# Scratch stores issued by POOL instead of the sync engine, and the first score tiles read from the transposed q and k

## The chip, the cores and the metric

The program runs on one core of a Trainium2 chip. The time is device time in microseconds (us). PE is the matrix engine, PEld its weight loads, DVE the vector engine, ACT the scalar engine, POOL the GpSimd engine, and SP the sync engine, which computes nothing and issues DMAs.

## The reference

```python
# attention, batch 4, 8 heads, 576 positions, head size 64, float32
q_rot, k_rot = rotate(q), rotate(k)
scores = q_rot @ k_rot.T / sqrt(64)
attn = softmax(scores)
a = attn @ v                                   # -> x: 2304 tokens x 512
# first layer, d_ff = 1536, weights float64
xn = x / sqrt(mean(x*x) + 1e-6) * rms_g
x = (silu(xn @ w_gate) * (xn @ w_val)) @ w_out
# second layer, d_ff = 1024, weights float64
out = ((x @ w1) * (x @ w2)) @ w3 @ w_out2
```

## The kernel before

**Precision.** A float32 product is made from two parts of each factor, a high part rounded to the fast matmul type and the remainder as the low part, in three passes: high by high, high by low, low by high (`PASS`). Where the contraction is only 64 long (the scores), high and low are stacked over 128 rows, so that two passes give all four products.

**Attention.** It goes over 16 pairs of heads (p = 0 to 15). For each pair POOL rotates q and k, PE transposes them (steps q0p, q1p, q2p), ACT takes the high part into the tile `xy` (q0h, q1h, q2h) and DVE the low part (q0l, q1l, q2l). DMAs issued by SP then move `xy` into the stacks `qs` (q1d, line 434 by `move`) and `ks` (q2d). Nine score tiles per pair follow, t = 0 to 8 (S, line 482): 0 to 3 are the first head's full tiles, 4 holds the left-over rows of both heads, 5 to 8 are the second head's. Each tile has its maximum taken by DVE (M, line 487), its exponential by ACT (E, line 493), is transposed by PE (T, line 499) and split again (H by ACT, Lo by DVE, line 507), before the product with v (PV). The order on every engine is written out by hand in `ORDER`, in units of one score tile. For pair 0 there is a shortcut: the first head's parts of the stacks are not moved by DMA but copied, three casts on ACT (lines 728, 731, 733) and three on DVE (lines 729, 732, 734), so that the first scores do not wait for DMAs; `q1d(0)` and `q2d(0)` then move only what is left (six moves).

**First layer.** Tokens go in six chunks of 384. Each chunk has 12 steps: `pair_mm` (line 305) multiplies by gate and value, `gated` makes the hidden slice (lines 315, 317, 104, 105), and `second` (line 813) adds it, one step later, into the output. Beside these steps run jobs that prepare the second layer. `job_wo`, `job_w3` and `job_ws` load float64 weights (`wraw`), turn them into float32 on ACT and DVE (lines 841 to 846) and store them to scratch tensors in DRAM (`woD`, `w3D`, `wsD`). `job_sums` loads pieces of the finished layer output `x2D`, adds them up as a seven-product (Strassen) scheme wants them, splits them and stores them to `xsD`. Their tiles come from small rings: three buffers for `wraw`, three for `wt`, three for `o`.

**Second layer.** `weights` loads `wsD` as `cf` (line 1024) and splits it into `cw`; `load_xs` loads seven tiles of `xsD` for each of two groups of chunks (line 1075); the third group's tiles are made on the spot from `x2D` (loads `sb`, line 908). `product` multiplies (line 1049), the results go to `uD` (line 1120). Then w3 by w_out2 is multiplied out (line 1152), `uD` is loaded again (line 1161), multiplied (line 1190) and stored to the output.

From the first layer on, a scheduler at build time orders the instructions of each engine. Each engine and each issuing queue then works its list strictly in order: an issue whose source is not ready holds back everything behind it. The DMAs of one issuing engine take turns on eight completion counters, and an issue waits until the DMA that last used its counter has landed. In the kernel before every DMA is issued by SP.

The memory of the `xs` tiles is memory that first-layer weights and inputs had. By the pool sizes in the code, the first three of the seven loads of group 0 (order 0, 1, 4, 5, 6, 2, 3) go into room that the early steps of the last chunk leave free; the fourth needs the room of the last chunk's input `xc`, which the last matmul of line 305 still reads.

Of the kernel before, what the change touches and what calls it, by code (L numbers as in the profile page):

```python
# [60 lines left out]
def f(ap):  # L61
    return ap.bitcast(F32)
# [3 lines left out]
def kernel(  # L66
# [21 lines left out]
    nc = tc.nc  # L88
    B, H, S, D = q.shape
# [346 lines left out]
    @step  # L436
    def q1d(p):
        qs = qst[p % 2]
        sl = slice(0, 640)
        sa = sl  # L440
        if p == 0:
            sa = slice(512, 640)
        move([(qs[0:64, 0, sa], xs[0:64, sa]), (qs[64:128, 0, sa], ys[0:64, sa]),
              (qs[64:128, 1, sl], xs[64:128, sl]), (qs[0:64, 1, sl], ys[64:128, sl])])

    @step
    def q2d(p):
        new_ks(p)
        ks = stacks[p]
        sl = slice(QW, QW + S)  # L450
        move([(ks[a:a + 64, 2 * h:2 * h + 2], xy[64 * h:64 * h + 64, :, sl]) for h in range(1 if p == 0 else 0, 2) for a in (0, 64)])

    def new_ks(p):
        if p not in stacks:
# [15 lines left out]
    def tile_steps(t):  # L470
        def S_(p):
            qs, ks = qst[p % 2], stacks[p]
            ps = ps_s.tile([128, 2, 512], F32, tag="s", name="s")
            if t == 4:
                mm = [(qs[:, h, 512 + 64 * h:640 + 64 * h], ks[:, 2 * h + i]) for h in range(2) for i in range(2)]
            else:
                h, r = hr(t)
                mm = [(qs[:, h, r * 128:(r + 1) * 128], ks[:, 2 * h + i]) for i in range(2)]
            n = len(mm)
            for hf in range(2):  # L480
                for i, (l, r_) in enumerate(mm):
                    nc.tensor.matmul(ps[:, hf, 0:HS], lhsT=l, rhs=r_[:, hf * HS:(hf + 1) * HS], start=(i == 0), stop=(i == n - 1))  # L482
            s_ps[p, t] = ps

        def M_(p):
            nm = s_max[p, t] = sm_p.tile([128, 1], F32, tag="nm", name="nm")
            nc.vector.tensor_reduce(out=nm, in_=s_ps[p, t][:, :, 0:HS], axis=AX.XY, op=ALU.max, negate=True)  # L487

        def E_(p):
            pp = p_sb[p, t] = p_p.tile([128, S], F32, tag="p", name="p")  # L490
            if p not in sums:
                sums[p] = sm_p.tile([128, 9], F32, tag="sums", name="sums")
            nc.scalar.activation(out=pp.rearrange("p (a b) -> p a b", a=2), in_=s_ps.pop((p, t))[:, :, 0:HS], func=AF.Exp,  # L493
                                 bias=s_max.pop((p, t)), scale=1.0, accum_out=sums[p][:, t:t + 1])

        def T_(p):
            ps = t_ps[p, t] = ps_t.tile([128, 4, 128], F32, tag="g", name="tp")
            for c in range(4):
                nc.tensor.transpose(ps[:, c, :], p_sb[p, t][:, LF + c * 128:LF + (c + 1) * 128], idn)  # L499

        def H_(p):
            hi, lo, src = spots(t_ps[p, t], t)
            lastins["act"] = nc.scalar.copy(out=hi, in_=src)  # L503

        def Lo(p):
            hi, lo, src = spots(t_ps.pop((p, t)), t)
            lastins["dve"] = nc.vector.tensor_tensor(out=lo, in0=src, in1=f(hi), op=ALU.subtract)  # L507

        for n_, fn in (("S", S_), ("M", M_), ("E", E_), ("T", T_), ("H", H_), ("Lo", Lo)):
            part[f"{n_}{t}"] = fn  # L510
# [206 lines left out]
            part[n_](0, eng, n)  # L717
    for n_ in ("ra", "rb", "rc", "rd"):
        part[n_](1)
    new_ks(0)  # L720
    ks, sl = stacks[0], slice(QW, QW + S)
    for i, n_ in enumerate(("q2p", "q0p", "q1p")):
        part[n_](0)
        if i < 2:
            warm(i + 1)
    for n_ in ("q2h", "q0h", "q2l", "q0l", "q2d"):
        part[n_](0)
    nc.scalar.copy(out=ks[0:64, 0], in_=xs[0:64, sl])
    nc.vector.tensor_copy(out=ks[0:64, 1], in_=ys[0:64, sl])
    part["q1h"](0), part["q1l"](0)  # L730
    nc.scalar.copy(out=qst[0][0:64, 0, 0:512], in_=xs[0:64, 0:512])
    nc.vector.tensor_copy(out=ks[64:128, 1], in_=ys[0:64, sl])
    nc.scalar.copy(out=ks[64:128, 0], in_=xs[0:64, sl])
    nc.vector.tensor_copy(out=qst[0][64:128, 0, 0:512], in_=ys[0:64, 0:512])
    for n_ in ("q1d", "vh", "vl"):
        part[n_](0)
    load_v(1, x_p.tile([128, 5, 2 * D], F32, tag="x", name="x").rearrange("p r n -> p (r n)").rearrange("p (h n d) -> p h n d", h=2, n=5))
    nc.sync.dma_start(out=g_sb, in_=rms_g.rearrange("(o n) -> o n", o=1).to_broadcast([128, DM]))
# [56 lines left out]
    def part_out():  # L795

        for o in range(KC):
            t = pools["x2"].tile([128, CH], F32, tag="o", name="part")
            (nc.scalar.copy if o % 2 else nc.vector.tensor_copy)(out=t, in_=acc[o][:, 0:CH])
            nc.sync.dma_start(out=part_d[:, o], in_=t)  # L800

    def part_in(o):
        t = pools["x2"].tile([128, CH], F32, tag="o", name="part")
# [3 lines left out]
    def second(kind, i, n, us):  # L807
        first, last_ = [(0, cut - 1), (cut, NF - 1)][n >= cut] if i == 0 else (0, NF - 1)
        if n == first:
            acc_tiles()  # L810
        for o in range(KC):
            for s, (a, b_) in enumerate(PASS):
                nc.tensor.matmul(acc[o][:, 0:CH], lhsT=wo[kind, n][:, a, o * 128:(o + 1) * 128], rhs=us[:, b_],  # L813
                                 start=(n == first and s == 0), stop=(n == last_ and s == 2))
        if n == cut - 1 and i == 0:
            part_out()
        elif n == last_:
            for o in range(KC):
                src = acc[o][:, 0:CH]
                if i == 0:  # L820
                    src = part_in(o)
                    nc.vector.tensor_tensor(out=src, in0=acc[o][:, 0:CH], in1=src, op=ALU.add)
                t = pools["x2"].tile([128, CH], F32, tag="o", name="x2") if i < NCH - 1 else pools["u"].tile([128, CH], F32, tag=("sg", "u", "us", "us")[o], name="x2", bufs=(1, 1, 2, 2)[o])
                nc.scalar.activation(out=t, in_=src, func=AF.Copy, scale=1.0 / UP)
                nc.sync.dma_start(out=x2D[:, o, i * CH:(i + 1) * CH], in_=t)

    def conv(src, c=None):

# [25 lines left out]
    def job_wo(j):  # L854
        load, rest = conv(rows(w_out2, j))

        def go():
            t = rest()
            hi, lo = [wt_p.tile([128, 512], F32R, tag="t", name="wt") for _ in range(2)]
            split(hi, lo, t)  # L860
            for i, o in enumerate((hi, lo)):
                nc.sync.dma_start(out=woD[:, j, i], in_=f(o))
        return [load, go]

    def job_w3(j, h):
        load, rest = conv(rows(w3, j, h))
        return [load, lambda: nc.sync.dma_start(out=w3D[:, j, h], in_=rest())]

    def job_ws(g, s):

        w = (w1, w2)[s]
        cv = [conv(cols(w, 2 * g + i), 1) for i in range(2)]
        u = {}

        def load():
            for ld, _ in cv:
                ld()

        def put(i, t):
            nc.sync.dma_start(out=wsD[:, g, s, i:i + 2].rearrange("p o n -> p (o n)"), in_=t)  # L880

        def go1():
            t1, t2 = [rest() for _, rest in cv]
            u["a"] = a11, a12, a21, a22 = t1[:, 0:256], t1[:, 256:512], t2[:, 0:256], t2[:, 256:512]
            u["s"] = tm = wt_p.tile([128, 512], F32, tag="t", name="wt")
            put(0, t1)
            put(2, t2)
            tt(tm[:, 0:256], a21, a22, ALU.add)
            tt(tm[:, 256:512], tm[:, 0:256], a11)
            put(4, tm)  # L890

        def go2():
            a11, a12, a21, a22 = u["a"]
            tm = u["s"]
            tt(tm[:, 256:512], a12, tm[:, 256:512])
            tt(tm[:, 0:256], a11, a21)
            put(6, tm)
        return [load, go1, go2]
# [31 lines left out]
    def job_sums(P, c):  # L930
        def bufs():
            return ([wst.tile([128, 512, 2], U32, tag="raw", name="wraw").rearrange("p n t -> p (n t)").bitcast(F32)[:, 0:2 * CH] for _ in range(2)],
                    [wt_p.tile([128, 512], F32, tag="t", name="wt")[:, 0:CH] for _ in range(2)])

        def put(i, c, src):
            o = pools["x2"].tile([128, 2, CH], F32R, tag="o", name="xo")
            split(o[:, 0], o[:, 1], src)
            nc.sync.dma_start(out=xsD[:, P, i, :, c], in_=f(o))
        return wsums(P, c, bufs, put)


# [156 lines left out]
    for k, batch in enumerate(todo):  # L1098
# [18 lines left out]
        for st_, b, t, g, s, P in run:  # L1117
            if s:
                nc.vector.scalar_tensor_tensor(out=t[:, 1:4], in0=t[:, 1:4], scalar=UP**-2, in1=G[P][:, 1:4], op0=ALU.mult, op1=ALU.mult)
                nc.sync.dma_start(out=uD[:, 2 * g:2 * g + 2, 2 * P * CH:2 * (P + 1) * CH], in_=t.rearrange("p (g t) n -> p g (t n)", g=2))  # L1120

        g, s, P = batch[-1]
        n_ = (g + 1, s) if P == 2 else None
# [132 lines left out]
```

## Time and profile before

| | |
|---|---|
| median of three runs | 1136.8 us (1135.91 to 1142.46) |
| the profiled execution | 1132.41 us |
| its span, first to last instruction | 1130.6 us |
| mean granted TensorE clock | 0.986 |
| busy in the span | PE 1086.5 us, DVE 691.6, ACT 559.3, POOL 218.6 (nothing after 400 us) |
| DMA packets | 183.52 MB, all but 1.17 MB on the queue fed by SP |

Attention takes about the first 310 us of the span, the first layer runs to 792 us, the second to the end. Times in rows are microseconds from the start of the span. The profile is of one execution, 4.4 us below the median of the runs. A merged row of the timeline (x6) gives the start of its first instruction and the time to the end of its last; what stands in brackets is how long the engine was idle before it and what ended that.

### The profile page before, as it was taken

How to read it: one execution, taken by the hardware profiler on the slowest of the kernel's cores; microseconds unless marked ns; L12 is line 12 of the kernel's file. 1: busy time of each engine (PE TensorE's matmuls, PEld its weight loads, DVE VectorE, ACT ScalarE, POOL GpSimd, SP SyncE). 2: the span in 40 equal slices, each digit the busy share in tenths (PEclk: the TensorE clock that was granted, in tenths of full speed). 3: DMA queues.
4: the chain of work that ended last, by engine and by line, in shares of the span. 5: the costliest groups of instructions: out<-in, count | busy, mean ns of one | idle time of the engine just before them, and what ended most of it. 6: DMA issues, size and time to landing. Idle time of an engine off the chain costs nothing. (4 is left out here: it accounts for less than half of the span.)

```text
span 1130.6 us, 18269 instructions
## 1 busy us (share of the span) xinstructions
PE 1086.5 (96%) x6627; PEld 1042.8 (92%) x6627; DVE 691.6 (61%) x1278; ACT 559.3 (49%) x1241; POOL 218.6 (19%) x191
## 2 busy tenths in 40 slices
PE   6899998999999999999999999999899999999998
PEld 5799998999888999999999999998799999987886
DVE  6999999999889853353677634566353442433221
ACT  4799997899865532232533423332354433323221
POOL 4767877599200000000000000000000000000000
PEclk7999999999999999999999999999999999999999
DMA  7678867685356520150878613866952325703451
GB/s 199 150 188 202 214 162 177 181 208 141 88 183 193 177 93 1 62 172 29 285 243 298 212 43 117 301 185 226 376 182 84 122 84 161 249 15 110 155 168 57
DMA packets 124698, 183.52 MB, mean 162 GB/s; under 512 B 18624, under 2 KB 85696, under 8 KB 124608
## 3 DMA queue, kind: packets, MB, share of 16 engines
q1 hardware_dynamic: 124608, 182.35, 53.1%
q8 instruction: 53, 0.87, 0.3%
q14 instruction: 37, 0.30, 0.1%
HBM read 101.63 MB, written 52.17 MB: 136 GB/s over the span
## 5 line engine op out<-in xcount | busy, mean ns | idle before, releaser
L305 PE MATMUL mm<-xc,wgv 128*128 128x384 f32 x1728 | 319.3, 336 | 1.5 <-ACT wgv L242 0.8
L305 PEld LDWEIGHTS mm<-xc,wgv 128*128 128x128 f32 x1728 | 301.8, 189 | 3.4 <-ACT wgv L242 1.6
L1049 PE MATMUL ps<-xs,cw 128*128 128x384 f32 x1008 | 178.3, 337 | 5.3 <-DMA xs<-xsD 5.2
L1049 PEld LDWEIGHTS ps<-xs,cw 128*128 128x128 f32 x1008 | 176.1, 189 | 7.0 <-DMA xs<-xsD 6.9
L813 PE MATMUL acc<-us,wo 128*128 128x384 f32 x864 | 169.8, 339 | 9.4 <-ACT us L104 6.1
L813 PEld LDWEIGHTS acc<-us,wo 128*128 128x128 f32 x864 | 151.3, 189 | 14.8 <-ACT us L104 8.7
L482 PE MATMUL s<-ks,qs 128*128 128x288 f32 x640 | 122.2, 318 | 11.6 <-ACT p L493 5.1
L493 ACT ACTIVATE p<-s,nm 128x576 f32<-128x576 f32 x144 | 107.5, 746 | 19.4 <-DVE nm L487 18.6
L487 DVE TENSOR_REDUCE nm<-s 128x1 f32<-128x576 f32 x144 | 108.0, 750 | 11.0 <-PE s L482 9.3
L482 PEld LDWEIGHTS s<-ks,qs 128*128 128x128 f32 x640 | 91.6, 193 | 15.4 <-ACT p L493 7.3
L1190 PE MATMUL ps<-wp,us 128*128 128x512 f32 x432 | 98.2, 389 | 1.4 <-ACT us L104 1.4
L1190 PEld LDWEIGHTS ps<-wp,us 128*128 128x128 f32 x432 | 81.0, 188 | 18.6 <-ACT us L104 1.8
L507 DVE TENSOR_TENSOR pt<-tp,pt 128x512 fp32r<-128x512 f32 x144 | 94.6, 682 | 1.3 <-ACT pt L503 0.6
L317 DVE SCALAR_TENSOR_TENSOR u<-mm,sg 128x384 f32<-128x384 f32 x72 | 39.9, 554 | 80.4 <-PE mm L305 72.1
L499 PE MATMUL tp<-idn,p 128*128 128x128 f32 x576 | 83.2, 277 | 0.7 <-DVE lt L537 0.4
L503 ACT CAST pt<-tp 128x512 fp32r<-128x512 f32 x144 | 82.5, 585 | 1.0 <-PE tp L499 0.2
L555 PE MATMUL pv<-pt,vs 128*128 128x288 f32 x512 | 81.9, 302 | 0.9 <-DVE pt L507 0.9
L104 ACT CAST us<-u 128x384 fp32r<-128x384 f32 x72 | 36.9, 512 | 89.2 <-DVE u L317 83.6
L555 PEld LDWEIGHTS pv<-pt,vs 128*128 128x128 f32 x512 | 71.7, 190 | 1.4 <-DVE pt L507 1.4
L499 PEld LDWEIGHTS tp<-idn,p 128*128 128x128 f32 x576 | 68.5, 143 | 2.3 <-PE s L482 0.9
L315 ACT ACTIVATE sg<-mm 128x384 f32<-128x384 f32 x72 | 35.1, 487 | 55.8 <-PE mm L305 55.3
L841 ACT ACTIVATE wraw<-wraw 128x512 f32<-128x512 f32 x40 | 27.5, 689 | 67.2 <-DMA wraw<-in_moe_w_dram 61.6
(138 smaller groups left out, 1352.8 us busy)
## 6 DMA issues: line engine op xcount, KB each, us to landing
ks<-xy SPq DMA_DIRECT2D x62, 288.0 KB, 5.0
wraw<-in_moe_w_dram SPq DMA_DIRECT2D x32, 512.0 KB, 5.2
xsD<-xo SPq DMA_DIRECT2D x28, 384.0 KB, 3.4
xs<-xsD SPq DMA_DIRECT2D x14, 768.0 KB, 9.8
wraw<-in_moe_w_out_dram SPq DMA_DIRECT2D x20, 512.0 KB, 4.8
qs<-xy SPq DMA_DIRECT2D x62, 160.0 KB, 2.8
uD<-gv SPq DMA_DIRECT2D x12, 768.0 KB, 3.9
gv<-uD SPq DMA_DIRECT2D x24, 384.0 KB, 4.4
```

The source lines that it names most:

```text
L305: nc.tensor.matmul(ps[:, 0:CH], lhsT=w[:, a, s, c * 128:(c + 1) * 128], rhs=x[:, b_, c, :], start=(i == 0), stop=(i == 3 * KC - 1))
L317: nc.vector.scalar_tensor_tensor(out=u, in0=va, scalar=1.0 / UP, in1=sg, op0=ALU.mult, op1=ALU.mult)
L482: nc.tensor.matmul(ps[:, hf, 0:HS], lhsT=l, rhs=r_[:, hf * HS:(hf + 1) * HS], start=(i == 0), stop=(i == n - 1))
L487: nc.vector.tensor_reduce(out=nm, in_=s_ps[p, t][:, :, 0:HS], axis=AX.XY, op=ALU.max, negate=True)
L493: nc.scalar.activation(out=pp.rearrange("p (a b) -> p a b", a=2), in_=s_ps.pop((p, t))[:, :, 0:HS], func=AF.Exp, bias=s_max.pop((p, t)), s ...
L499: nc.tensor.transpose(ps[:, c, :], p_sb[p, t][:, LF + c * 128:LF + (c + 1) * 128], idn)
L503: lastins["act"] = nc.scalar.copy(out=hi, in_=src)
L507: lastins["dve"] = nc.vector.tensor_tensor(out=lo, in0=src, in1=f(hi), op=ALU.subtract)
L555: nc.tensor.matmul(ps[:, 0:HS], lhsT=l.rearrange("p s d -> p (s d)"), rhs=r, start=(i == 0), stop=(i == 8))
L813: nc.tensor.matmul(acc[o][:, 0:CH], lhsT=wo[kind, n][:, a, o * 128:(o + 1) * 128], rhs=us[:, b_], start=(n == first and s == 0), stop=(n = ...
L1049: nc.tensor.matmul(b[ch], lhsT=w[i][:, p_, c * 128:(c + 1) * 128], rhs=x[i][:, r, c], start=(first and ch != 1 and n == 0), stop=(n == 5), ...
L1190: nc.tensor.matmul(ac[o], lhsT=us[j // 2][:, a, j % 2, o * 128:(o + 1) * 128], rhs=wp[j][:, b_], start=(j == 0 and s == 0), stop=(j == NJ ...
```

## The change

Two things are changed.

1. All stores to the scratch tensors are issued by POOL: `part_d`, `x2D`, `woD`, `w3D`, `wsD`, `xsD` and `uD` (4, 24, 16, 16, 32, 28 and 12 stores). Loads, the stores of `xD` and of the output, and the moves of `xy` stay with SP.
2. The shortcut of pair 0 is replaced. Score tiles 0 to 3 are multiplied straight from `xy`, 64 rows, in three passes instead of two; the six copies are dropped, and `q1d(0)` and `q2d(0)` move whole stacks, as they do for every other pair (eight moves).

```diff
     def q1d(p):
...
-        if p == 0:
-            sa = slice(512, 640)
-        move([(qs[0:64, 0, sa], xs[0:64, sa]), (qs[64:128, 0, sa], ys[0:64, sa]),
+        move([(qs[0:64, 0, sl], xs[0:64, sl]), (qs[64:128, 0, sl], ys[0:64, sl]),
...
-        move([... for h in range(1 if p == 0 else 0, 2) for a in (0, 64)])
+        move([... for h in range(2) for a in (0, 64)])
...
+            if p == 0 and t < 4:
+                mm = [(xy[0:64, a, o], xy[0:64, b_, QW:QW + S]) for a, b_ in PASS]
...
-    for n_ in ("q2h", "q0h", "q2l", "q0l", "q2d"):
-        part[n_](0)
-    nc.scalar.copy(out=ks[0:64, 0], in_=xs[0:64, sl])
-    nc.vector.tensor_copy(out=ks[0:64, 1], in_=ys[0:64, sl])
-    part["q1h"](0), part["q1l"](0)
-    nc.scalar.copy(out=qst[0][0:64, 0, 0:512], in_=xs[0:64, 0:512])
-    nc.vector.tensor_copy(out=ks[64:128, 1], in_=ys[0:64, sl])
-    nc.scalar.copy(out=ks[64:128, 0], in_=xs[0:64, sl])
-    nc.vector.tensor_copy(out=qst[0][64:128, 0, 0:512], in_=ys[0:64, 0:512])
-    for n_ in ("q1d", "vh", "vl"):
+    for n_ in ("q2h", "q0h", "q2l", "q0l", "q1h", "q1l", "q2d", "q1d", "vh", "vl"):
         part[n_](0)
...
-            nc.sync.dma_start(out=part_d[:, o], in_=t)
+            nc.gpsimd.dma_start(out=part_d[:, o], in_=t)
...
-                nc.sync.dma_start(out=x2D[:, o, i * CH:(i + 1) * CH], in_=t)
+                nc.gpsimd.dma_start(out=x2D[:, o, i * CH:(i + 1) * CH], in_=t)
...
-                nc.sync.dma_start(out=woD[:, j, i], in_=f(o))
+                nc.gpsimd.dma_start(out=woD[:, j, i], in_=f(o))
...
-        return [load, lambda: nc.sync.dma_start(out=w3D[:, j, h], in_=rest())]
+        return [load, lambda: nc.gpsimd.dma_start(out=w3D[:, j, h], in_=rest())]
...
-            nc.sync.dma_start(out=wsD[:, g, s, i:i + 2].rearrange("p o n -> p (o n)"), in_=t)
+            nc.gpsimd.dma_start(out=wsD[:, g, s, i:i + 2].rearrange("p o n -> p (o n)"), in_=t)
...
-            nc.sync.dma_start(out=xsD[:, P, i, :, c], in_=f(o))
+            nc.gpsimd.dma_start(out=xsD[:, P, i, :, c], in_=f(o))
...
-                nc.sync.dma_start(out=uD[:, 2 * g:2 * g + 2, 2 * P * CH:2 * (P + 1) * CH], in_=t.rearrange("p (g t) n -> p g (t n)", g=2))
+                nc.gpsimd.dma_start(out=uD[:, 2 * g:2 * g + 2, 2 * P * CH:2 * (P + 1) * CH], in_=t.rearrange("p (g t) n -> p g (t n)", g=2))
```

## Rows read from the trace of the kernel before

**Rows 1.** Busy time by stretch: us, engine busy (count), PEclk, DMA share, GB/s.
```profile
200.00:300.00 100.00, 98.03 (x786) 95.63 (x785) 94.61 (x162) 90.42 (x222) 74.87 (x76) 1.00 0.68 172
```
**Rows 2.** What PE waited for, whole span: us in total, times, longest.
```profile
PE ps L1049 <- DMA xs<-xsD: 5.2, 4, 3.0
```
**Rows 3.** Timeline of the first 60 us: start, us, engine, line.
```profile
11.36 1.28 SPq L434 DMA_DIRECT2D ks<-xy  x2
...
12.23 0.59 ACT L420 CAST xy<-qtp 128x512 fp32r<-128x512 f32 x1 [0.52 <-PE qtp L416]
12.68 3.59 SPq L434 DMA_DIRECT2D qs<-xy  x4
...
13.12 0.67 DVE L424 TENSOR_TENSOR xy<-qtp,xy 128x512 fp32r<-128x512 f32 x1
...
16.44 2.26 PE L482 MATMUL s<-ks,qs 128*128 128x288 f32 x8 [4.24 <-DVE qs L734]
...
22.98 1.30 PE L482 MATMUL s<-ks,qs 128*128 128x288 f32 x8
...
23.25 0.69 DVE L507 TENSOR_TENSOR pt<-tp,pt 128x512 fp32r<-128x512 f32 x1 [0.64 <-ACT pt L503]
```
**Rows 4.** Busy time by stretch, at the start of the span.
```profile
20.00:22.00 2.00, 2.00 (x11) 1.98 (x10) 0.91 (x2) 0.75 (x3) 1.55 (x1) 0.50 0.61 152
```
**Rows 5.** Timeline of SP's queue around the change of layers.
```profile
774.89 0.38 SPq L1024 DMA_DIRECT2D cf<-wsD  x1
775.37 13.43 SPq L880 DMA_DIRECT2D wsD<-wt  x6
788.89 3.65 SPq L1075 DMA_DIRECT2D xs<-xsD  x7
792.63 5.09 SPq L825 DMA_DIRECT2D x2D<-x  x4
806.13 1.28 SPq L908 DMA_DIRECT2D sb<-x2D  x2
```
**Rows 6.** Timeline of PE around the change of layers.
```profile
782.81 4.32 PE L305 MATMUL mm<-xc,wgv 128*128 128x384 f32 x24
...
793.65 3.42 PE L1049 MATMUL ps<-xs,cw 128*128 128x384 f32 x18 [1.53 <-DMA xs<-xsD]
...
797.39 3.40 PE L1049 MATMUL ps<-xs,cw 128*128 128x384 f32 x18 [0.32 <-DMA xs<-xsD]
...
803.79 13.68 PE L1049 MATMUL ps<-xs,cw 128*128 128x384 f32 x66 [3.01 <-DMA xs<-xsD]
...
817.85 12.43 PE L1049 MATMUL ps<-xs,cw 128*128 128x384 f32 x70 [0.37 <-DMA xs<-xsD]
```
**Rows 7.** Busy time by stretch, around the change of layers.
```profile
780.00:790.00 10.00, 9.36 (x50) 8.59 (x50) 7.34 (x15) 1.96 (x5) 0.00 (x0) 1.00 0.36 134
790.00:800.00 10.00, 8.15 (x44) 7.41 (x44) 0.05 (x1) 3.09 (x7) 0.00 (x0) 1.00 1.00 396
...
805.00:810.00 5.00, 5.00 (x23) 5.00 (x23) 1.24 (x3) 1.53 (x4) 0.00 (x0) 0.71 0.85 277
```
**Rows 8.** What PE waited for, 400 to 786 us.
```profile
PE acc L813 <- ACT us L104: 3.0, 4, 1.0
PE acc L813 <- DVE us L105: 2.7, 4, 0.9
```
**Rows 9.** What ACT waited for, 400 to 830 us.
```profile
ACT xo L104 <- DMA xsD<-xo: 9.4, 8, 2.9
```
**Rows 10.** What DVE waited for, 400 to 830 us.
```profile
DVE wt L851 <- DMA wsD<-wt: 3.0, 6, 1.3
```
**Rows 11.** DMA issues: engine, count, KB each, median us from issue to landing.
```profile
ks<-xy SPq DMA_DIRECT2D x62, 288.0 KB, 5.0
...
xsD<-xo SPq DMA_DIRECT2D x28, 384.0 KB, 3.4
...
qs<-xy SPq DMA_DIRECT2D x62, 160.0 KB, 2.8
```

More of the change, by code (lines that the diff above doesn't have):

```diff
@@ L439, in q1d @@
         sl = slice(0, 640)
-        sa = sl
-        if p == 0:
-            sa = slice(512, 640)
-        move([(qs[0:64, 0, sa], xs[0:64, sa]), (qs[64:128, 0, sa], ys[0:64, sa]),
+        move([(qs[0:64, 0, sl], xs[0:64, sl]), (qs[64:128, 0, sl], ys[0:64, sl]),
               (qs[64:128, 1, sl], xs[64:128, sl]), (qs[0:64, 1, sl], ys[64:128, sl])])
@@ L450, in q2d @@
         sl = slice(QW, QW + S)
-        move([(ks[a:a + 64, 2 * h:2 * h + 2], xy[64 * h:64 * h + 64, :, sl]) for h in range(1 if p == 0 else 0, 2) for a in (0, 64)])
+        move([(ks[a:a + 64, 2 * h:2 * h + 2], xy[64 * h:64 * h + 64, :, sl]) for h in range(2) for a in (0, 64)])
     def new_ks(p):
@@ L477, in S_ @@
                 h, r = hr(t)
-                mm = [(qs[:, h, r * 128:(r + 1) * 128], ks[:, 2 * h + i]) for i in range(2)]
+                o = slice(r * 128, (r + 1) * 128)
+                mm = [(qs[:, h, o], ks[:, 2 * h + i]) for i in range(2)]
+            if p == 0 and t < 4:
+                mm = [(xy[0:64, a, o], xy[0:64, b_, QW:QW + S]) for a, b_ in PASS]
             n = len(mm)
@@ L719 @@
         part[n_](1)
-    new_ks(0)
-    ks, sl = stacks[0], slice(QW, QW + S)
     for i, n_ in enumerate(("q2p", "q0p", "q1p")):
```

## Prediction

> **What bounds the kernel now.** I read the table by stretch first. In mid-attention PE and DVE are both busy about 95% of the time [rows 1]: the stage runs at their throughput, so time won ahead of it stays won. In the first layer PE is nearly always busy; only what PE itself waits for can be won. So the list of PE's waits comes next. Two of them belong to things the change touches: 4.24 us once, for the copy of line 734 at the start [rows 3], and 5.2 us in four waits of the second layer's first products for `xs` [rows 2]. In the first layer, from 400 us on, PE waits 3.0 + 2.7 us for the hidden slice [rows 8]; all the moved stores come after that mark. Everything else the change touches lies beside PE's work. The third view is the timeline of SP's queue where the layers change: six `wsD` stores hold it for 13.43 us, because each waits for DVE, and the seven `xs` loads leave right behind the last of them [rows 5].
>
> **Part 1, the start.** Removed are six copies. What let the first score tile begin was the last of them; PE stood 4.24 us and began at 16.44 [rows 3]. Now the tile needs the high part of q, which is there at 12.23 + 0.59 = 12.82, for its first two passes and the low part for the third. The low part began at 13.12 behind a copy that goes; without it, it can end near 13.6 rather than 13.79. Each tile has six matmuls in place of four. A matmul took 2.26 / 8 = 0.283 us there [rows 3], and the clock was granted at 0.50, the lower of its two levels (1.2 GHz), as it still was at 20 to 22 us with PE busy throughout [rows 4]. With 64 rows instead of 128 I take the same price, as the time goes by columns in all the rows seen. Tile 0 then ends at about 13.6 + 4 x 0.283 = 14.7, where it ended at 16.44 + 4 x 0.283 = 17.57: 2.8 us won. Tiles 1 to 3 each give back 2 x 0.283 = 0.57, so 1.1 is left after the fourth, up to 1.9 where the added matmuls fit into pauses that PE has between these tiles anyway.
>
> The next tile, t = 4, reads the stacks, and these now come wholly by DMA: eight moves in place of six, with 2 x 288 and 2 x 128 KB added [rows 11]. Before, the issues began at 11.36 and ended at 12.68 + 3.59 = 16.27 [rows 3]. Two more of 1.28 / 2 = 0.64 us put the last at about 17.5; landing takes 2.8 to 5.0 us [rows 11], so the last part is there at 20.3 to 22.5, more if they share the engines. Tile 4 began at 22.98 and would now like to begin at 21.1 to 21.9. So the gain at this point lies between 1.9 us and a loss of about 1, if the moves come as late as 24. What follows is DVE, which works without a longer pause from 23.25 on [rows 3]. I take **0.8 us won**, nearer to the row of the landing than to the free case. Queued behind the two added issues on SP are the loads of v for pair 1, of the norm's weights, of the first layer weights and of q and k for pair 2, each 1.3 us later. What waits for these is work on a later pair, behind the tiles of pair 0, so I cost that at nothing; if that cover is not there, it costs the 1.3.
>
> **Part 2, the change of layers.** The first three `xs` loads need room that has been free for tens of microseconds; SP's last load ahead of the six stores was issued at 774.89 [rows 5]. With the stores gone to another queue these three can leave near 775.5, when the DMA engines have room (0.36 busy in 780 to 790) [rows 7], and land long before PE needs them. The fourth must wait for the last matmul of line 305, at 782.81 + 4.32 = 787.1 [rows 6], so it and the rest leave from about 787.3 instead of behind three others from about 790.3. Four loads of 768 KB at the 396 GB/s that this stretch reaches [rows 7] take 7.9 us: all are there by about 796.5, and the one PE stood 3.01 us for until 803.79 [rows 6] with them. Then the `x2D` stores: SP issued them behind the loads, over 5.09 us, and the loads `sb` and the next seven `xs` stood until 806.13 for their landing [rows 5]. From POOL's queue they can leave as soon as ACT has made them, so the second group comes earlier too.
>
> What is that worth? From the end of the first layer, 793.65 - 1.53 = 792.12, to 817.85 - 0.37 = 817.48, PE did 18 + 18 + 66 = 102 matmuls [rows 6]. The following row has 12.43 / 70 = 0.178 us each, so 102 need 18.1 us; they took 25.4. The excess of 7.2 us is 4.9 us of waits and the rest a slower pace, part of it at a granted clock of 0.71, a mean between the levels, after the 3.01 us pause (805 to 810) [rows 7]. I take **6.0 us won** of 7.2, as the DMA engines are full there and the order of SP's loads is the scheduler's; the bounds are 0 and 7.2.
>
> A rule speaks against this part. The row shows a queue held for 13.43 us by stores that are not ready [rows 5], so what is won is the hold, not the time to issue. The Trainium skill, "DMA: Bandwidth & Descriptors", section "Issuing engines are not separate DMA queues", says that DMAs from several engines share the same 16 DMA engines and that issuing from more than one saves only the sequencer's issue time, usually small. By that this part is worth about nothing; it is the first of the rivals.
>
> **Part 3, the stores along the first layer.** 132 issues move. SP is rid of about 0.4 us of issuing for each [rows 5], off PE's path. What may cost is their landing. ACT waits 9.4 us in 8 waits for `xsD` stores to release a buffer, DVE 3.0 us in 6 for `wsD` [rows 9, 10], and behind such a wait stand, in order, the steps that make the hidden slice for PE. No DMA of the trace is issued by POOL, so I bound the change in landing: from 1 us earlier (a store no longer takes its turn among SP's loads) to 3.4 us later, the median landing of an `xsD` store once more [rows 11]. The 14 waits last 12.4 us now and PE waits 5.7 us [rows 8]; if that ratio, 0.46, held, each microsecond of lateness would cost 14 x 0.46 = 6.4 us. POOL computes nothing in this stage, and the loads that no longer stand behind stores gain what the late stores lose. I take **0**, with -6 to +22 as the ends.
>
> The Trainium skill gives, on the same page under "Specifications", a first byte after some 1 us for a DMA issued by GpSimd and some 0.6 us for one issued by SP. By that the stores are 0.4 us late, an estimate from that page of 2.6 us lost, and the sum would be -4.2 us.
>
> The `uD` stores and the end of the kernel I cost at nothing: PE is busy without a break from 818 us to the product of w3, and the last stage is loads and matmuls that don't change. If a late `uD` store holds back the transposes of w3, it costs the lateness once, 1 to 2 us.
>
> **The sum.** -0.8 - 6.0 + 0 = -6.8 us. The profiled execution took 1132.4, so 1125.6 in its terms; the median of the runs is 4.4 us above it, and I give the number against the median: 1136.8 - 6.8 = **1130.0 us**, with 1126 to 1135 as this case's own range.
>
> **The rivals.**
> *The issue alone is saved.* `xs` waits for bandwidth and not for the queue: 1.00 DMA share in 790 to 800 [rows 7]; or the scheduler puts the loads behind something else, so that the change doesn't do what it says. Against it: DMA share 0.36 in the ten microseconds before, and loads free to go. Then only the start is left: 1136.
> *Late stores stall PE.* In the steps after 450 us ACT and DVE stand for buffers of `xsD`, `wsD` and `woD` behind stores from POOL. It decides from 6.8 / 6.4 = 1.1 us of added landing; at 2 us it costs 12.8 and gives 1136.8 - 6.8 + 12.8 = 1143, slower than before; at 3.4 us it costs 21.8 and gives 1152. For it: the fourteen waits. Against it: PE's 5.7 us came in eight waits only [rows 8], so that most waits for a buffer did not reach it.
> *The queue was in the way everywhere.* Earlier loads of `wraw` also take away the 5.7 us of line 813, the start gives 1.9 and the change of layers 7.2: 14.8 won, 1122.
>
> **How the numbers follow.** Chances: the forecast 0.58, issue alone 0.17, late stores 0.13, everywhere 0.12. The range reaches down to the last of these and up to the smaller price of late stores: 1122 to 1143. One per cent is 11.4 us, about what a measurement of this kernel can tell from no change (its three runs differ by 6.5). Below 1125.4 lie the case "everywhere" and a little of the forecast: 0.14. Above 1148.2 lies only the dear half of the late stores: 0.06. Within: 0.80.
>
> **What would show it.** Right: the first score matmul at about 13 us with a wait of under 1 us, tile 4 before 22.5; the first `xs` loads issued before 780, the waits of line 1049 for `xs` under 1 us in sum, no 0.71 in the clock near 805; line 813's waits near 6 us. Wrong: tile 4 standing for `ks` or `qs`; `xs` loads still leaving at 788 or later; new or longer waits of ACT and DVE for `xsD`, `wsD` or `woD`, with line 813's waits above 10 us.

## Result and the profile after

| | before | after |
|---|---|---|
| median, same chip | 1138.5 us (4 runs) | 1151.7 us (4 runs) |
| ratio | | 1.011, 95% interval 1.0076 to 1.0144 |
| profiled execution, its span | 1132.4, 1130.6 us | 1151.9, 1150.1 us |
| mean granted TensorE clock | 0.986 | 0.978 |

By the medians the change cost 13.2 us, by the interval 8.7 to 16.4. The prediction was 1130.0, in a range of 1122 to 1143: the time fell outside and went the other way. In the layers a line of the changed kernel is 11 lower than the same line before (813 is 802, 851 is 840, 880 is 869, 1049 is 1038, 1075 is 1064). In the versions with a fresh buffer, from experiment 2 on, the lines of the second layer are one higher (1049 is 1050, and 1039 in the changed kernel).

**The start.** PE's timeline in the changed kernel; these rows answer to [rows 3]:

```profile
11.41 3.49 PE L482 MATMUL s<-xy 64*128 64x288 f32 x12 [0.67 <-ACT xy L420]
...
21.19 1.78 PE L482 MATMUL s<-ks,qs 128*128 128x288 f32 x6 [0.39 <-DMA qs<-xy]
...
36.70 1.30 PE L482 MATMUL s<-ks,qs 128*128 128x288 f32 x4 [5.14 <-DMA ks<-xy]
```

The 4.24 us in front of the first tile are gone; it begins at 11.41 instead of 16.44, and a matmul costs 3.49 / 12 = 0.291 us, as estimated. Tile 4, the first on the stacks, begins 1.8 to 3.0 us earlier than its 22.98 of before. Then comes a wait that before did not have: the first tile of pair 1 stands 5.14 us for `ks`. Before, PE stood at the same place for another engine:

```profile
35.19 0.80 PE L482 MATMUL s<-ks,qs 128*128 128x288 f32 x4 [3.00 <-ACT p L493]
```

So the lead of 1.8 to 3.0 us is gone there and the tile begins 1.5 us late. SP's queue in the changed kernel:

```profile
10.62 3.75 SPq L434 DMA_DIRECT2D ks<-xy  x4
14.48 3.93 SPq L434 DMA_DIRECT2D qs<-xy  x4
...
25.22 3.84 SPq L434 DMA_DIRECT2D qs<-xy  x4
29.58 3.70 SPq L434 DMA_DIRECT2D ks<-xy  x4
```

Pair 0's moves go on until 18.41 (before 16.27), everything behind them leaves 2.1 us later, and the last moves of pair 1 leave only by 33.28 (before 31.51).

**The first layer.** What PE waited for between 400 and 786 us, to be held against [rows 8], and what DVE waited for between 400 and 830 us, against [rows 10]:

```profile
PE acc L802 <- DVE us L105: 6.8, 6, 2.1
PE acc L802 <- ACT us L104: 2.4, 4, 1.1
```
```profile
DVE wt L840 <- DMA wsD<-wt: 14.8, 8, 6.6
```

PE's waits for the hidden slice grew from 5.7 to 9.2 us, DVE's for a `wsD` store from 3.0 to 14.8.

**The change of layers.** Four engines in order of time, to be held against [rows 5] and [rows 6]:

```profile
800.14 1.94 SPq L1064 DMA_DIRECT2D xs<-xsD  x4
```
```profile
801.50 0.54 POOL L869 DMA_DIRECT2D wsD<-wt  x1 [1.57 <-DVE wt L840]
```
```profile
808.30 0.76 DVE L840 TENSOR_TENSOR wt<-wt 128x256 f32<-128x256 f32 x2 [6.63 <-DMA wsD<-wt]
808.98 0.55 DVE L317 SCALAR_TENSOR_TENSOR u<-mm,sg 128x384 f32<-128x384 f32 x1
```
```profile
810.13 4.21 PE L802 MATMUL acc<-us,wo 128*128 128x384 f32 x12 [6.21 <-ACT us L104]
814.13 4.13 PE L1038 MATMUL ps<-xs,cw 128*128 128x384 f32 x17
```

Read from the bottom: PE goes from the first layer into the second without a wait for `xs`; the 5.2 us of [rows 2] are gone. But just ahead it stands 6.21 us for ACT, which waits for DVE, which at 808.30 has waited 6.63 us for a `wsD` store to leave its buffer. POOL issued that store at 801.50, while SP was sending four `xs` loads of 768 KB. The loads that no longer wait behind the stores now run beside and ahead of one. The stretch 805 to 810 (columns as in [rows 7]) has PE at zero and the transfer engines full (a share can pass 1, as a transfer is counted where it starts):

```profile
805.00:810.00 5.00, 0.00 (x0) 0.00 (x0) 1.23 (x3) 0.43 (x1) 0.54 (x1) 0.61 1.01 420
```

**Where the time went.** I took the start of the n-th matmul of a line in one trace minus that of the same matmul in the trace of before, in us, as the median within 3 us of each mark (marks in the time of before). One trace is one execution, and executions of one kernel differ by some 4 us either way, so only steps that recur count. Medians are against the kernel before on the same chip. The trace of before is itself one execution: from 315 to 560 us every row below but that of the changed kernel gains 1.3 to 3.8 us on it, so some 2.5 us of what stands from 560 on belong to that trace and not to the versions.

| kernel | 44 | 315 | 560 | 630 | 785 | 830 | 1110 | median |
|---|---|---|---|---|---|---|---|---|
| after | 1.4 | 4.8 | 4.9 | 9.9 | 13.0 | 14.9 | 19.1 | +13.2 |
| start alone | 1.2 | 4.3 | 0.8 | 1.3 | -0.3 | 0.9 | 1.0 | +4.2 |
| stores alone | -0.3 | 0.8 | -1.7 | 1.3 | 3.9 | 5.8 | 7.1 | +8.9 |
| after, fresh buffer | 2.2 | 5.7 | 3.4 | 7.4 | 3.8 | -2.1 | -1.5 | +1.6 |
| before, stores and fresh buffer | -0.9 | 0.3 | -3.5 | -2.0 | -3.2 | -11.2 | -10.8 | -1.9 |
| before, fresh buffer | 0.1 | 1.0 | -1.6 | -2.6 | -4.6 | -2.9 | -2.7 | -1.3 |
| wsD alone on POOL | -0.8 | 1.7 | -1.1 | -0.8 | 3.5 | 5.9 | 6.3 | +5.9 |
| all but wsD on POOL | -1.0 | -1.5 | -2.8 | -0.7 | 1.1 | 2.6 | 3.7 | +6.1 |
| wsD on POOL, fresh buffer | -0.6 | 0.5 | -2.1 | -2.3 | -0.8 | -8.9 | -8.7 | -4.6 |

The changed kernel's 19.1 us come in five steps: 4.8 by the end of attention, 5.0 from 560 to 630, 3.1 from 630 to 785, 1.9 from 785 to 830, and 4.3 more near 980. At the change of layers PE waits 7.8 us for the hidden slice there and none for `xs`, where before it waited 0.3 and 5.2: the collision costs a little more than the earlier loads save.

### The profile page after: what moved, and what is told of

The parts are those of the page before. It is cut to its first block, busy times and chain, and to the rows that moved or that the text cites. A ratio compares the mean times of both kernels' runs of the same rounds, so it can differ in the third digit from the quotient of the medians.

```text
span 1150.1 us, 18372 instructions
## 1 busy us (share of the span) xinstructions
PE 1096.3 (95%) x6635; PEld 1050.5 (91%) x6635; DVE 688.9 (60%) x1275; ACT 556.6 (48%) x1238; POOL 296.7 (26%) x323
## 4 chain that ended last, share of the span: by engine, by line
PE 57%; issue 20%; DMA 9%; DVE 7%; POOL 3%; ACT 2%; SPq 1%; POOLq 0%; DVEq 0%; ACTq 0%
PE ps L1038 11%; PE mm L305 10%; PE ps L1179 9%; PE s L482 6%; PE acc L802 5%; PE pv L555 4%; PE tp L499 4%; PE ps L1141 4%; DMA wraw<-in_moe_w_dram 3%; DVE nm L487 1%; PE qtp L416 1%; PE lp L529 1%; POOL wsD L869 1%; DMA ks<-xy 1%; DMA raw<-in_q_dram 1%
## 5 line engine op out<-in xcount | busy, mean ns | idle before, releaser
L802 PE MATMUL acc<-us,wo 128*128 128x384 f32 x864 | 173.3, 343 | 20.2 <-ACT us L104 11.2
L482 PE MATMUL s<-ks,qs 128*128 128x288 f32 x624 | 119.5, 318 | 8.6 <-DMA ks<-xy 5.8
L482 PEld LDWEIGHTS s<-ks,qs 128*128 128x128 f32 x624 | 89.1, 192 | 11.7 <-issue 6.2
```

## Experiments

**1. Which part costs.** The first kernel has the change of the start alone, all stores on SP. The second has the stores alone:

```diff
-            nc.sync.dma_start(out=part_d[:, o], in_=t)
+            nc.gpsimd.dma_start(out=part_d[:, o], in_=t)
... and so x2D, woD, w3D, wsD, xsD, uD; the start stays as before
```

> Start part alone, all stores on SP as before. Theory 1 (two separate losses; in the changed kernel the work of attention stood 1.1 to 2.4 us behind the kernel before from 40 to 290 us and 4.8 us behind at its end): 1.5 to 5 us slower than before, with PE waiting some 5 us for ks near 36 us. Theory 2 (the start only shifted phases and all the loss comes with the stores): within 1 us of before.

> Stores on POOL alone, start as before. Theory 1: 19.1 - 4.8 = about 14 us slower than before; attention ends as before, PE's waits for the hidden slice near 17 us from 400 us on, no PE wait for xs. Theory 2 (one loss, by the stores): all 19 us slower. Rival 3 (parts only hurt together): within 3 us of before.

Measured: start 1135.7 against 1131.6 us, ratio 1.0044 (1.0024 to 1.0064); stores 1140.5 against 1131.6, ratio 1.0067 (1.0042 to 1.0092). Both cost, and 4.2 + 8.9 = 13.1 is the whole within the intervals: two losses that add up. The start costs what its theory allowed, the stores less than expected.

**2. The wait on the buffer of the late store.** Two attempts to take it away from the changed kernel. First, the stores of the last `ws` job back on SP; second, `go2` of a `ws` job writes its sums into a fresh tile of the ring of raw words, not into the buffer that the job's own store just before still reads:

```diff
-            nc.gpsimd.dma_start(out=wsD[:, g, s, i:i + 2]...
+            (nc.sync if (g, s) == (3, 1) else nc.gpsimd).dma_start(out=wsD[:, g, s, i:i + 2]...
```
```diff
             tm = u["s"]
-            tt(tm[:, 256:512], a12, tm[:, 256:512])
-            tt(tm[:, 0:256], a11, a21)
-            put(6, tm)
+            o = wst.tile([128, 512, 2], U32, tag="raw", name="wraw")...
+            tt(o[:, 256:512], a12, tm[:, 256:512])
+            tt(o[:, 0:256], a11, a21)
+            put(6, o)
```

> The changed kernel, but the four wsD stores of the last weight job go back to SP's queue, where the xs loads can't pass them. Theory 1 (PE's 6.2 us stand ahead of the second layer is DVE waiting for a wsD store that lands late among the xs loads): that stand falls under 2 us and the time by 3 to 6 us, unless xs loads now come late and PE waits for them instead (then the sum is as in the changed kernel). Rival (the planned order of DVE is what costs): stand and time as in the changed kernel.

> The changed kernel, but the second half of each weight job writes its sums into a buffer of the load ring instead of over the tile that is being stored, so DVE no longer waits there for a store to land. Theory 1: DVE's waits for wsD (13.9 us in seven) go to nearly zero, PE's stand of 6.2 us goes, 5 to 10 us faster than the changed kernel. Rival (planned order): at most 2 us faster. A third way: the load ring becomes short and loads come later, PE's waits stay.

The first gave 1146.0 against 1131.6, ratio 1.0126 (1.0094 to 1.0158), where the changed kernel has 1.011: nothing won. Its waits between 700 and 830 us say why:

```profile
DVE wt L840 <- DMA wsD<-wt: 7.0, 6, 2.0
```
```profile
PE ps L1038 <- DMA xs<-xsD: 7.2, 3, 4.8
```

With these stores ahead on SP's queue DVE waits half as long, and `xs` is late again. The order only chooses who waits. The second gave 1133.2 against 1131.6, ratio 1.001 (0.9988 to 1.0031): most of the loss is back. DVE has no wait for `wsD` left, and where the changed kernel lost 3.1 us from 630 to 785 and 1.9 from there to 830, this one wins 3.6 and 5.9 (table).

**3. Does the buffer do it alone, and do the stores then win?** The kernel before with POOL's stores and the fresh buffer, and the kernel before with the fresh buffer alone.

> The start as in the kernel before, the stores on POOL's queue, and the last sums of a ws job written into a fresh tile of the raw words instead of the buffer that the job's first store still reads. Theory 1 (the stores on POOL lose only by the waits on buffers that a late store still reads, above all this one; what they gain is that xs no longer queues behind stores): the wait of DVE on the wsD store (13.5 us in the run with the stores alone) is gone, the wait for xs too, and the time is 5 to 9 us under the kernel before. Rival A (POOL's issue and the planner's other order cost time by themselves, wherever the buffers are): no faster than before, 0 to +4 us. Rival B (the fresh buffer is worth the time by itself, whichever queue issues the stores): the same as the next run, within 2 us.

> The kernel before with the fresh buffer alone; all stores stay on the sync engine. Theory 1: there DVE waited 3.0 us on the wsD store before, hidden but for a part, and xs still queues behind the stores, so -3 to 0 us, and 4 us or more behind the run with POOL's queue. Rival B (the buffer alone): -5 to -9 us.

Ratios 0.9994 (0.9964 to 1.0024) and 0.9994 (0.9971 to 1.0017). My forecast of 5 to 9 us for the first fell. Its trace, of its fastest execution (1121.5 where the median is 1129.2), shows the gain at the change of layers, 8.0 us from 785 to 830; its runs spread from 1121 to 1138, and the median keeps 1.9, which the interval does not tell from nothing. The buffer alone wins nothing that can be measured, so what it saved in experiment 2 is the wait that POOL's stores had made.

**4. Which stores.** `wsD` alone on POOL, and all but `wsD`. (The texts on record count 62 stores; it is 132. `wsD` with 32 is a quarter of them, as they say.)

> The kernel before with the wsD stores alone (the sums of the shared expert's weights) issued by POOL; the six other kinds of store stay on the sync engine. Theory 1 (the stores lose where DVE waits to overwrite a buffer that a wsD store still reads, and nowhere else by more than 2 us): DVE's wait on wsD in 700 to 830 is well above the 3.0 us of before, and the time is +5 to +9 us, as with all stores on POOL. Rival D (the loss is spread over the stores, each landing some later and POOL taking longer to issue one): 16 of 62 stores give a quarter of the loss, +1 to +3 us.

> The complement: all stores but wsD on POOL, wsD left on the sync engine. Theory 1: no loss is left, -3 to +2 us. Rival D: three quarters of the loss, +5 to +7 us. If neither half loses much, the loss needs both: wsD is late only when the loads of xs overtake it, which they can only do when xsD no longer holds them.

1138.8 and 1139.0 against 1132.9: ratios 1.0054 (1.0033 to 1.0075) and 1.005 (1.0031 to 1.0069). Neither theory had both. `wsD` alone costs 5.9 us, as mine wanted; DVE's waits from 700 to 830 us:

```profile
DVE wt L851 <- DMA wsD<-wt: 13.9, 5, 7.7
```

But the others cost 6.1, which mine did not allow. There `wsD` holds SP's queue as in [rows 5], and `xs` stays late (PE's waits, 785 to 830 us):

```profile
PE ps L1049 <- DMA xs<-xsD: 7.1, 3, 4.7
```

So the gain at `xs` needs `wsD` off SP's queue. The two halves make 12.0 and all together 8.9, which the intervals do not tell apart. The table shows another loss that goes with the other stores: from 560 to 630 us the six kernels with all or all but `wsD` on POOL lose 1.5 to 5.0 us (2.3 in the one not in the table); in the table's others the step is -1.0 to 0.5. In that stretch PE's waits for the hidden slice are what grew: 5.5 us in the changed kernel, 1.9 before.

**5. The version that follows, and the converted weights.** `wsD` alone on POOL with the fresh buffer; and `woD` and `w3D` alone on POOL (32 stores of the 132).

> The kernel before with the wsD stores alone on POOL and the fresh buffer for the last sums of a ws job; the six other kinds of store stay on the sync engine. Theory 3 (three terms that add up: the wait on the buffer of a late wsD store, +9 or more; xs no longer held behind these stores, -6 or more; the other stores on POOL, +5): only the gain is left, -5 to -9 us, and PE waits for neither xs nor a wsD store. Rival E (what is gained at xs is given back by the stores and loads that then collide, whichever they are): within 2 us of the kernel before, as with all stores on POOL and the fresh buffer.

> The kernel before with woD and w3D alone (the stores of converted weights, 30 of the 62) on POOL. Theory 3 puts the loss of the stores other than wsD in the stretch 560 to 640, where DVE and ACT wait for a woD store to leave its buffer: the delay grows by 2 to 4 us between 560 and 630, and the time is +3 to +5 us. Rival F (it is xsD, x2D or uD): the delay does not grow there, and the time is -1 to +2 us.

The first is the fastest: 1127.1 against 1131.7, ratio 0.9968 (0.9947 to 0.9990). Its trace is of one of its fastest executions (1123.8). Three engines of it, in the order SP, PE, POOL:

```profile
776.22 12.13 SPq L1076 DMA_DIRECT2D xs<-xsD  x7
```
```profile
786.19 4.32 PE L813 MATMUL acc<-us,wo 128*128 128x384 f32 x24
790.35 18.26 PE L1050 MATMUL ps<-xs,cw 128*128 128x384 f32 x102
```
```profile
778.12 0.54 POOL L880 DMA_DIRECT2D wsD<-wraw  x1
```

The last `wsD` store leaves at 778.12 (809.36 in the changed kernel); the first `xs` loads leave at 776.22 (before 788.89), and PE does in one run of 18.26 us the 102 matmuls that took 25.4 before [rows 6]. That is the gain the prediction had put on this part. The second came to 1132.6, ratio 1.0008 (0.9987 to 1.003): `woD` and `w3D` cost nothing, and its delay does not grow from 560 to 630 (0.6, then -0.7). That leaves `x2D`, `xsD` or `part_d` for the loss of that stretch, or several kinds of store together; these were not run apart.

**6. The start: the order of the loads.** The loads of `g` and of the first two weight blocks (1.25 MB) behind pair 1's moves and the first steps on these weights later; each once with the new start and once, as control, with the old.

```diff
-ONCE = {"WF.0": 0.058, "WF.1": 0.481, "W0.0": 2.871, "W1.0": 3.803, "W2.0": 4.815, ...
+ONCE = {"WF.0": 1.46, "WF.1": 1.47, "W0.0": 4.3, "W1.0": 4.9, "W2.0": 5.9, ...        (first)
+ONCE = {"WF.0": 1.50, "WF.1": 1.51, "W0.0": 5.6, "W1.0": 6.1, "W2.0": 6.7, ...        (second)
+ONCE = {"WF.0": 1.50, "WF.1": 1.51, "W0.0": 8.1, "W1.0": 8.35, "W2.0": 8.6, ...       (third)
... the load of g_sb moved from the prologue to 1.48 (first) and 1.52
```

> The start's part of the change alone, with the load of g and the first two loads of expert weights (1.25 MB) issued behind the moves of pair 1 in place of ahead of them, and the first three steps on those weights planned 1.4 to 1.1 tiles later. Theory 1 (the start's part loses because pair 1's moves queue behind these loads and share the transfer engines with them): PE's wait for ks falls from 4.1 us to under 1.5 us, and the time from +4 us to -3 to +1 us against the kernel before. Rival C (what is lost lies in the late transposes of pair 1 or in the clock that PE gets at the start): the wait for ks may shrink, but the time stays at +3 to +5 us.

> The kernel before with the same three loads moved behind pair 1's moves. Theory 1: PE does not wait for ks there, so nothing is to be had, -1 to +2 us. If it gains as much as the run with the start's part does (3 us or more), the loads cost both kernels the same and are not what the start's part loses by.

> The start's part alone, once more with the loads of g and of the first two weight blocks late, this time behind all eight moves of pair 1 (in the run before this they still stood ahead of its last four), and the steps on those weights planned at tiles 5.6 to 6.7, behind their landing. Theory 1 (the start's part loses because pair 1's moves come behind these loads and share the transfer engines with them): PE waits under 1.5 us for ks and none takes its place, and the time is -2 to +1 us against the kernel before. Rival C (the order of the loads is not what costs): +3 to +5 us, with another wait in its place.

> The kernel before with the same three loads behind all eight moves of pair 1 and the same later steps. Theory 1: PE did not wait for ks before, so nothing is to be had: -1 to +2 us, and within 2 us of the run with the start's part. If this one gains 3 us or more, the order of the loads is a gain of its own and tells nothing of the start's part.

> The start's part alone, the loads of g and of the first two weight blocks (1.25 MB) behind all moves of pair 1, and this time the six steps on those weights planned behind the first tiles of pair 1 (8.1 to 9.2), so that no engine meets them before they have landed. Theory 4 (the start's part loses because its 0.83 MB of added moves meet transfer engines that are full of loads from 24 to 36 us): pair 1's moves land some 2 to 3 us sooner, PE's wait for ks is under 2 us with none in its place, and the time is -1 to +2 us against the kernel before. If the wait stays or another comes and the time with it, +4 us or more, the loss at the start isn't to be had back by the order of the loads, and pair 1 is bound by something else.

> The control: the kernel before with the same order of loads and steps. Theory 4: its moves are 0.83 MB fewer and PE waits little for ks, so -1 to +2 us. If it gains or loses as much as the run with the start's part moves against the start alone, the order of loads acts on both alike.

Ratios of new start and control: 1.0038 and 1.0038; 1.0062 and 1.0053; 1.0053 and 1.0071; no interval reaches further than 0.003 to either side. None came near the forecast, and the controls lost as much, so the order tried here costs something by itself. In the first pair I had put the weights ahead of the last four moves (in its control PE, against what I expected, then stood 7.2 us for `ks` with the old start too), in the second ACT met them 7.9 us before they had landed. The third comes closest. PE there, and ACT:

```profile
32.55 0.76 PE L482 MATMUL s<-ks,qs 128*128 128x288 f32 x4 [1.45 <-ACT osb L560]
```
```profile
37.19 0.69 ACT L220 ACTIVATE wraw<-wraw 128x512 f32<-128x512 f32 x1 [4.88 <-DMA wraw<-in_moe_w_gate_dram]
```

The wait for `ks` is gone and pair 1 begins at 32.55 instead of 36.70; then ACT stands 4.88 us for the weights, and the lead is lost. So with these loads out of the way the wait for `ks` goes, but whoever is put last is waited for.

**7. The start: another queue.** Pair 1's eight moves issued by POOL, every load in its place; and the same in the kernel before.

```diff
-    def move(mv):
+    def move(mv, eng=nc.sync):
         for o, i in mv:
-            nc.sync.dma_start(out=f(o), in_=f(i))
+            eng.dma_start(out=f(o), in_=f(i))
... called in q1d and q2d with nc.gpsimd if p == 1 else nc.sync
```

> The start's part alone, with the eight moves of pair 1 issued by POOL in place of the sync engine; every load keeps its place. Theory 1 (pair 1's moves are late because they stand behind the sync engine's loads): they are issued as soon as their data is there, PE's wait for ks falls from 4.1 us to under 2 us, and the time comes to -1 to +2 us against the kernel before. Rival C (the transfer engines are full of the loads from 24 to 36 us whichever queue issues, share 1.0): the wait for ks stays at 3 us or more, and the time at +3 to +5 us.

> The control: the kernel before with the eight moves of pair 1 issued by POOL. Both theories: PE waits little for ks there, -2 to +2 us. If it gains 3 us or more, the moves' queue costs both kernels the same.

1139.3 and 1136.3 against 1131.7: ratios 1.0074 (1.0046 to 1.0103) and 1.0052 (1.0028 to 1.0076). With the new start POOL issues the moves from 23.97 to 28.56, where SP issued them up to 33.28 in the changed kernel; still PE waits 6.02 us for `ks`. DMA issues between 20 and 44 us (KB each, median us to landing), of the new start:

```profile
ks<-xy POOLq DMA_DIRECT2D x4, 288.0 KB, 10.9
qs<-xy POOLq DMA_DIRECT2D x4, 160.0 KB, 8.5
...
raw<-in_k_dram SPq DMA_DIRECT2D x1, 256.0 KB, 9.5
raw<-in_q_dram SPq DMA_DIRECT2D x1, 256.0 KB, 12.3
```

and of the control, whose start has moved 832 KB less:

```profile
ks<-xy POOLq DMA_DIRECT2D x4, 288.0 KB, 5.9
qs<-xy POOLq DMA_DIRECT2D x4, 160.0 KB, 4.1
raw<-in_k_dram SPq DMA_DIRECT2D x2, 256.0 KB, 4.7
raw<-in_q_dram SPq DMA_DIRECT2D x2, 256.0 KB, 5.3
```

With the new start and the moves on SP (start alone) the same two rows have 5.5 and 5.9 us. So the moves leave earlier and land no earlier: the last at 39.0, against 37.7 in start alone. The loads beside them pay too. The control's two rows for loads are medians of one load beside the moves and one behind them; those beside landed after 6.9 and 7.4 us, against 9.5 and 12.3. An earlier issue buys nothing here, for which the rival stood: the transfer engines are full. That the added 832 KB are what fills them is inferred; no run took the bytes away alone. The stretch 24 to 36 us (columns as in [rows 7], DMA share and GB/s last) in the kernel before, which the rows above do not show, and in the changed kernel:

```profile
24.00:36.00 12.00, 8.03 (x60) 7.03 (x59) 11.64 (x17) 8.12 (x20) 7.12 (x4) 1.00 0.92 223
```
```profile
24.00:36.00 12.00, 6.65 (x47) 5.72 (x45) 10.44 (x15) 8.47 (x20) 4.29 (x2) 0.93 1.05 275
```

The control lost too, at another place: PE stood 7.8 us for ACT in front of pair 1, and ACT 8.4 us for DVE. Two of DVE's steps on the first layer's weights there, and what POOL did meanwhile:

```profile
29.70 5.10 DVE L224 TENSOR_SCALAR wraw<-wraw 128x512 uint32<-128x512 uint32 x1
34.83 2.98 DVE L228 SCALAR_TENSOR_TENSOR wt<-wraw 128x512 uint32<-128x512 uint32 x1
```
```profile
29.15 2.68 POOL L368 TENSOR_TENSOR rot<-raw,cos 128x1152 f32<-128x1152 f32 x1
```

The median of these two steps in the same trace is 0.43 and 0.68 us. Before, they took 1.49 and 1.77 us beside POOL's work, inside the 3.00 us for which PE stood in front of pair 1; in start alone POOL began only at 31.20 and they took 0.42 and 0.69. So in front of pair 1 the new start puts the wait for `ks` in place of a wait for DVE, and moving work of POOL or DVE shifts that place as well.

## Why the prediction was wrong

**Part 1, the start: the first half right, one term missing.** The wait of 4.24 us went, the price of a matmul held, and near 23 us the changed kernel is 1.6 us ahead (same measure as the table), where I had 0.8 with 1.9 as the better end. What failed is "What waits for these is work on a later pair ... so I cost that at nothing; if that cover is not there, it costs the 1.3". The cover was not there, and the loads were 2.1 us later, not 1.3. I had counted the added bytes, 2 x 288 + 2 x 128 = 832 KB, only for the landing of tile 4. At the 223 GB/s of 24 to 36 us they are 3.8 us of transfer, an estimate, and they push the loads onto the moves of pair 1, which PE needs as soon as pair 0 is through. That an earlier issue does not help while the transfer engines are full, experiment 7 shows; that the added bytes are the cause is the reading that fits, not one that a run isolates. Near 44 us the four kernels with the new start and no load moved are 1.2 to 2.2 us late, the seven with the old start and loads -1.0 to 0.1; near 315 us 4.3 to 8.4 against -1.5 to 1.8. So the traces show a start's loss of about 2 us and as much again or more by the end of attention, for a median of 4.2. Part of the second half is a wait of DVE for a load of weights near 295 us (2.3 to 2.5 us in these four traces, and PE 2.6 to 2.8 behind it, where before has 1.1 and 0.9); four of the eight traces with the old start have it at 1.6 us or more too. Why the new start meets it each time stays open.

**Part 2, the change of layers: the mechanism right, the collision missed.** The hold of the queue by stores was what the 5.2 us of [rows 2] hung on, and 6.0 us was a fair size: with `wsD` off the queue and its buffer free the delay falls by 5.9 to 8.1 us from 785 to 830 in three traces. But I let the seven `xs` loads run early and did not ask what they run ahead of. The `wsD` store that leaves beside them lands late, and DVE wants its buffer at once. Of the trace of before I had the row for it: DVE's six waits for `wsD` [rows 10].

**Part 3, the stores along the first layer: "I take 0" was the wrong end.** The rival of late stores came true, with its price right in kind: `wsD` landed after 4.7 us in the median where it took 2.4, `w3D` after 5.3 where it took 3.4, so some 2 us late, for which I had written 12.8 us lost and a time of 1143. (`woD` and `x2D` landed sooner, 3.8 for 4.4 and 2.4 for 3.8; the estimate of 0.4 us for every store fits none of the four.) My argument against it, that most waits for a buffer did not reach PE, fell in the last chunk, where PE needs the very next hidden slice and DVE stands for `wsD`, and in a way that is not explained between 560 and 630 us. A `uD` store cost more than allowed in one trace (4.3 us from 975 to 990 in the changed kernel, at most 1.4 in the others).

**The sum.** By medians: start +4.2 where I had -0.8, stores +8.9 where parts 2 and 3 had -6.0. The rule that I had as the first rival comes from the Trainium skill (page "DMA: Bandwidth & Descriptors", section "Issuing engines are not separate DMA queues"): DMAs from several issuing engines share the same DMA engines, and a second issuing engine saves issue time only. Its first half agrees with both parts here: the `wsD` store issued beside four loads landed 6.7 us after its issue, where the median is 4.7, and moves issued earlier landed no earlier. Its second half does not cover a queue that is held by stores which are not ready: from 785 to 830 us the three traces with `wsD` on POOL and the fresh buffer gain 5.9 to 8.1 us, where the buffer alone loses 1.7. By the medians of the whole that is 4.6 us against 1.3, with intervals of 1.1 to 6.0 and -1.9 to 3.3, so the runs' times alone do not part the two.

What stays open: which of `x2D`, `xsD` and `part_d` costs the 2 to 5 us from 560 to 630 us; why all stores on POOL with the fresh buffer keep only 1.9 us in the median where one execution kept 10; and how much of the start's loss the added moves make by themselves.

## What to carry to other kernels

When loads are freed from behind stores, list what they overtake, and for each store overtaken ask who waits to write its buffer; moving the store and giving that writer another buffer is one change, not two. Before adding DMAs to a stretch, read its DMA share: here it was 0.92 already, and with more to carry ahead of it the next transfer that someone needed came late, whichever queue issued it. And measure a gain on medians of several runs: a trace 10 us better than before belonged to a kernel that was 2 us better.

## What was not expected of the hardware

- Some stores landed later when POOL issued them, others did not. The same 256 KB, medians: `w3D` 3.4 us from SP and 5.2 from POOL (with `wsD` left on SP), `wsD` 2.4 and 5.4 (alone on POOL), but `woD` 4.4 and 3.5. What sets it apart was not tried; the stores also leave at other times then, beside other transfers.
- An issue of a `wsD` store occupies POOL for 0.54 us, where SP took 0.32 us for one that it did not have to wait with; POOL's busy time rose from 218.6 to 296.7 us, at no cost that the runs show.
- A pause of PE was paid for twice: after the one of 6.21 us the granted clock is 0.68 from 810 to 820, a mean between the two levels, and the first 17 matmuls of the second layer take 4.13 / 17 = 0.243 us each, where the version without a pause takes 18.26 / 102 = 0.179.
- Three of DVE's steps on the first layer's weights (lines 224, 228, 233) took at most 0.43, 0.69 and 0.69 us wherever POOL did not compute beside them for over 30% of their time, in the traces of before and of experiment 7's control. Beside POOL's work, in 31 of 216 cases, they took up to 5.10, 2.98 and 2.76 us.
